# Strassen's seven products in place of eight, two blocks of 384 columns, in the second expert layer of a fused fp32 kernel

## The chip, the cores and the metric

The kernel runs on one core of a Trainium2 chip. The metric is the time of one execution on the device in microseconds (us). TensorE (PE in the rows, PEld for its weight loads) multiplies matrices into PSUM, which has eight banks here named bank_61 to bank_68; VectorE (DVE) and ScalarE (ACT) work element by element; GpSimd (POOL) does little here; SyncE (SP) issues all DMA transfers.

## The reference

Block-and-window attention over 2 x 768 tokens with 8 heads of 64 gives x of 1536 tokens by 512. Two dense layers follow, each with its own weights:

```python
def _moe_ref(x, w_in, w_out):            # w_in 512 x 2048, w_out 2048 x 512
    h = x @ w_in
    sp = np.where(h > 20.0, h, np.log1p(np.exp(np.minimum(h, 20.0))))
    return ((h * np.tanh(sp)) @ w_out).astype(np.float32)

def _moe2_ref(x, w_a, w_b, w_out):       # w_a, w_b 512 x 1536, w_out 1536 x 512
    a = x @ w_a
    b = x @ w_b
    return (a * b @ w_out).astype(np.float32)
```

All arithmetic is fp32. The weights arrive as 64-bit floats.

## The kernel before

Every fp32 product is made of three matmuls. Each operand is split into a rounded high part and a rest (`XH` and `XL` for x; high and low halves of a weight slot), and high x high, low x high and high x low are added up in PSUM. A split is always a ScalarE cast (the high part) and a VectorE subtraction (the rest).

The tokens stand in blocks 0 to 3 of 256, 256, 512 and 512 tokens; blocks 0 and 1 are mostly taken together, so a step handles 512 tokens. The layers' hidden columns are taken in chunks of 128: 16 for the first layer (`NC1`), 12 for the second (`NC2`). A visit is a token group with a range of chunks (`visits1`, `visits2`), and a step is one chunk of a visit. The stages run one after the other on TensorE: attention to about 84 us, mixed with the first visits; the first layer to about 335 us; then the second layer.

A step of the second layer (`step2`) computes a and b with 12 matmuls each: four pieces of the 512 input dimensions times three (line L811, in `x_product`). ScalarE copies a out of PSUM (L906), VectorE multiplies it with b, which it reads in PSUM (L907), ScalarE casts the product (L355, the line of the helper `copy`) and VectorE subtracts (L910). Two steps later 12 matmuls with w_out (L923) add the chunk to o, which stays in four PSUM banks for a whole visit and is copied or added at the visit's end (L944), and then stored. In the first layer L840 is the Mish activation, L843 its subtraction, and L858 the matmuls with w_out.

`load_w` fetches a weight tile of 128 x 512 (64-bit), and turns it into fp32 with integer instructions: ScalarE multiplies the high words by a power of two with Copy (L656), VectorE shifts the low words (L658), puts both together (L661) and puts in the sign (L664), and then the split follows (L355, L672). Each tile is converted once.

The order of all instructions is set before the program is built: `Plan.emit` takes the list of operations with their due times and estimated costs and puts out, engine by engine, the ready operation with the earliest key. On the chip each engine follows its own list, and semaphores hold it where data or a buffer isn't ready.

Of the kernel before, what the change touches and what calls it, by code (L numbers as in the profile page):

```python
# [232 lines left out]
def attention_mish_moe_bilinear_moe(  # L233
# [72 lines left out]
    RND = top[0]  # L306
    T_S = [take(512) for _ in range(NT)]
    T_L = [take(512) for _ in range(NT)]
    Y0, Y1 = take(KC * n_blk[0]), take(KC * n_blk[1])
    stage_o = [take(1024) for _ in range(NST)]  # L310
    SK = WIN + S + WIN
    kt_o = [take(SK) for _ in range(NP)]
    YP = [Y0, Y1, kt_o[0], None]
    assert kt_o[-1] + SK >= YP[2] + KC * n_blk[2]
    OP = [Y0, Y1, None, YP[2]]
# [15 lines left out]
    n_ext = max(top[0] - EXT, 1024 * N_EXT)  # L331
    assert EXT + n_ext <= TOT, EXT + n_ext
    ext_slots = [EXT + 1024 * i for i in range(n_ext // 1024)]
# [302 lines left out]
    free_slots = []  # L636
# [3 lines left out]
    def load_w(first, kind, c):  # L640
        free_slots.sort()
        t_free, o = free_slots.pop(0)
        w_at[kind, c] = o
        key = max(first - 9.0, t_free + 0.5)
        ext = [("ext",)] if o >= EXT else []
        _, so = nxt("stage", stage_o)
        kd = key - 4.0
        kd = w_dma.get((kind, c), kd)
        if BITS64:
            raw = ar(so, 512, 2)  # L650
            dma(kd, ar(so, 1024).bitcast(U32), w_dram[kind][c].bitcast(U32), w=[sb(so, 1024)],
                nbytes=P * 4096)
            f, hw = raw[:, :, 0], raw[:, :, 1]
# [4 lines left out]
            dve(key, 512, lambda env: nc.vector.tensor_scalar(  # L658
                out=f.bitcast(U32), in0=f.bitcast(U32), scalar1=29, scalar2=None,
                op0=ALU.logical_shift_right), fast=True, r=[sb(so, 1024)], w=[("f", so)])  # L660
            dve(key, 512, lambda env: nc.vector.scalar_tensor_tensor(  # L661
                out=f.bitcast(U32), in0=hw.bitcast(U32), scalar=3, in1=f.bitcast(U32),
                op0=ALU.logical_shift_left, op1=ALU.bitwise_or), r=[("hw", so), sb(so, 1024)], w=[("f", so)])
# [3 lines left out]
        else:  # L667
            f = ar(so, 512)
# [10 lines left out]
    def w_all(kind, c):  # L679
        o = w_at[kind, c]  # L680
        return lambda: (r32(ar(o + 512, 512)), r32(ar(o, 512)))

    def w_key(kind, c):
        return sb(w_at[kind, c], 1024)

# [323 lines left out]
```

## Time and profile before

| | |
|---|---|
| median of three runs | 630.74 us (630.29 to 633.08) |
| span of the profiled execution | 628.0 us; the page gives no other time for it |
| TensorE busy | 616.7 us, 98% |
| VectorE busy | 319.4 us, 51% |
| ScalarE busy | 263.1 us, 42% |
| second layer on TensorE | 335.41 to 623.74 us |

The span runs from the first to the last instruction of the profiled execution; a run's time is measured around the whole execution. A matmul's duration includes its way through the array, and matmuls overlap, so their pace is read from the starts. A row's duration of a VectorE or ScalarE instruction likewise overlaps a little with the next.

### The profile page before, as it was taken

To read this page: it belongs to the slowest core of one execution; us is meant where nothing else is said; L and a number is where in the kernel's file an instruction comes from. 1 tells how busy PE (TensorE), PEld (TensorE's weight loads), DVE (VectorE), ACT (ScalarE), POOL (GpSimd) and SP (SyncE) were. 2 spreads that over 40 slices of the span, in tenths; PEclk is the share of its full clock that TensorE was granted. 3 is DMA by queue.
4 is the path that set the end of the run, shared out by engine and by line. 5 is a ranking of instruction groups with operands and counts; after the bars stand their busy time and mean duration, and the time that the engine had idled before them with its cause. 6 is when DMAs were issued, how large, how long until landed. Compare 5 with 4: busy or idle time off the path is not lost.

```text
span 628.0 us, 9873 instructions
## 1 busy us (share of the span) xinstructions
PE 616.7 (98%) x3975; PEld 512.7 (82%) x3975; DVE 319.4 (51%) x741; ACT 263.1 (42%) x571; POOL 6.7 (1%) x34
## 2 busy tenths in 40 slices
PE   7899999999999999999999999999999999999997
PEld 4688988888888888888888888888888888888885
DVE  6989999998851311179898311115731111113112
ACT  5889989766632321256664112114521112111110
POOL 3000000000000000000000000000000000000000
PEclk8979999999999999999999999999999999999999
DMA  8997433445420000025542000002400001000101
GB/s 301 345 311 236 149 88 103 169 167 193 171 73 1 0 1 1 2 77 191 199 171 99 2 1 0 2 0 78 157 2 0 1 0 68 1 0 19 48 1 67
DMA packets 20633, 54.83 MB, mean 87 GB/s; under 512 B 1804, under 2 KB 4876, under 8 KB 20588
## 3 DMA queue, kind: packets, MB, share of 16 engines
q1 hardware_dynamic: 20588, 54.21, 25.2%
q8 instruction: 31, 0.51, 0.4%
q14 instruction: 14, 0.11, 0.1%
HBM read 50.07 MB, written 3.15 MB: 85 GB/s over the span
## 4 chain that ended last, share of the span: by engine, by line
PE 94%; ACT 4%; DMA 1%; issue 0%; DVE 0%; SPq 0%
PE bank L811 50%; PE bank L858 20%; PE bank L923 16%; PE bank L601 2%; PE bank L530 2%; PE bank L589 2%; ACT attn L557 2%; DMA attn<-in_qT_dram 1%; PE bank L534 1%; ACT rounded L355 0%; ACT arena L656 0%; ACT L840 0%; ACT L557 0%; PE bank L407 0%; PE bank L462 0%
## 5 line engine op out<-in xcount | busy, mean ns | idle before, releaser
L811 PE MATMUL bank<-rounded 128*128 128x512 f32 (+1 forms) x1068 | 239.1, 378 | 0.5 <-ACT arena L840 0.5
L811 PEld LDWEIGHTS bank<-rounded 128*128 128x128 f32 x1068 | 192.4, 188 | 38.1 <-ACT arena L840 0.7
L355 ACT CAST rounded<-arena 128x512 fp32r<-128x512 f32 (+1 forms) x131 | 81.1, 625 | 187.4 <-PE bank L923 125.9
L811 PE MATMUL bank<-rounded,wext 128*128 128x512 f32 x432 | 102.8, 389 | 0.0
L858 PE MATMUL bank<-rounded 128*128 128x512 f32 (+1 forms) x456 | 98.5, 364 | 0.0
L811 PEld LDWEIGHTS bank<-rounded,wext 128*128 128x128 f32 x432 | 81.1, 188 | 16.8
L907 DVE TENSOR_TENSOR arena<-arena,bank 128x512 f32<-128x512 f32 x36 | 24.7, 687 | 128.2 <-PE bank L811 128.1
L858 PEld LDWEIGHTS bank<-rounded 128*128 128x128 f32 x456 | 77.9, 189 | 13.7 <-issue 0.2
L843 DVE TENSOR_TENSOR rounded<-arena,rounded 128x512 fp32r<-128x512 f32 (+1 forms) x53 | 33.8, 637 | 72.6 <-ACT rounded L355 72.6
L923 PE MATMUL bank<-rounded 128*128 128x512 f32 x288 | 69.0, 389 | 0.0
L923 PEld LDWEIGHTS bank<-rounded 128*128 128x128 f32 x288 | 54.1, 188 | 11.2
L910 DVE TENSOR_TENSOR rounded<-arena,rounded 128x512 fp32r<-128x512 f32 x36 | 24.9, 692 | 66.3 <-ACT rounded L355 59.1
L656 ACT ACTIVATE arena<-arena 128x512 f32<-128x512 f32 x68 | 46.2, 684 | 16.2 <-DMA arena<-in_w_out_dram 7.6
L906 ACT COPY arena<-bank 128x512 f32<-128x512 f32 x36 | 21.2, 588 | 73.3 <-PE bank L811 73.3
L661 DVE SCALAR_TENSOR_TENSOR arena<-arena 128x512 uint32<-128x512 uint32 x68 | 47.0, 691 | 6.9 <-ACT arena L656 4.0
L840 ACT ACTIVATE arena<-bank 128x512 f32<-128x512 f32 (+1 forms) x53 | 29.4, 557 | 44.2 <-PE bank L811 44.0
L664 DVE SCALAR_TENSOR_TENSOR arena<-arena 128x512 uint32<-128x512 uint32 x68 | 46.9, 690 | 1.0
L858 PE MATMUL bank<-rounded,wext 128*128 128x512 f32 x180 | 43.2, 389 | 0.0
L557 ACT ACTIVATE attn<-attn 128x120 f32<-128x120 f32 x96 | 36.8, 385 | 8.7 <-DVE attn L551 8.6
L858 PEld LDWEIGHTS bank<-rounded,wext 128*128 128x128 f32 x180 | 33.8, 188 | 7.0
L672 DVE TENSOR_TENSOR rounded<-arena,rounded 128x512 fp32r<-128x512 f32 x47 | 32.2, 688 | 11.7 <-ACT rounded L355 11.4
L923 PE MATMUL bank<-wext,rounded 128*128 128x512 f32 x144 | 34.3, 389 | 0.0
(69 smaller groups left out, 385.7 us busy)
## 6 DMA issues: line engine op xcount, KB each, us to landing
arena<-in_w_out_dram SPq DMA_DIRECT2D x28, 512.0 KB, 3.4
arena<-in_w_in_dram SPq DMA_DIRECT2D x16, 512.0 KB, 3.7
arena<-in_w_a_dram SPq DMA_DIRECT2D x12, 512.0 KB, 3.2
arena<-in_w_b_dram SPq DMA_DIRECT2D x12, 512.0 KB, 3.3
arena<-in_kT_dram SPq DMA_DIRECT2D x8, 384.0 KB, 6.1
attn<-in_v_dram SPq DMA_DIRECT2D x4, 768.0 KB, 6.1
out_dram<-arena SPq DMA_DIRECT2D x12, 256.0 KB, 2.1
attn<-in_qT_dram SPq DMA_DIRECT2D x5, 512.0 KB, 6.1
```

The lines of the kernel that those rows point to most:

```text
L355: alts = [("ACT", act_us(n), lambda env: nc.scalar.copy(out=dst(env), in_=src(env))), ("DVE", dve2_us(n) if fast else dve_us(n), lambda en ...
L557: act(key, SW + 90, lambda env, x=x: nc.scalar.activation(out=s[:, x, :], in_=s[:, x, :], func=AF.Exp, scale=-1.0, bias=negm[:, x:x + 1], ...
L656: act(key, 512, lambda env: nc.scalar.activation(out=hw, in_=hw, func=AF.Copy, scale=2.0 ** -112), r=[sb(so, 1024)], w=[("hw", so)])
L661: dve(key, 512, lambda env: nc.vector.scalar_tensor_tensor(out=f.bitcast(U32), in0=hw.bitcast(U32), scalar=3, in1=f.bitcast(U32), op0=ALU. ...
L664: dve(key, 512, lambda env: nc.vector.scalar_tensor_tensor(out=f.bitcast(U32), in0=hw.bitcast(U32), scalar=0x80000000, in1=f.bitcast(U32), ...
L672: dve(key, 512, lambda env: nc.vector.tensor_sub(out=r32(ar(o, 512)), in0=f, in1=ar(o + 512, 512)), r=[sb(o + 512, 512), ("f", so), sb(so, ...
L811: nc.tensor.matmul(like(dst, b), lt, rt, start=(j == 0), stop=(j == 3 * KC - 1))
L840: act(ka, n, lambda env: nc.scalar.activation(out=g, in_=hp(env), func=AF.Mish), w=[hn, sb(lo, n)], free=[hn], table="mish")
L843: dve(ka, n, lambda env: nc.vector.tensor_sub(out=r32(gl), in0=g, in1=gh), r=[sb(lo, n), sb(ho, n)], w=[sb(go, n)])
L858: nc.tensor.matmul(yp, lt, r32(rt), start=(fst and j == 0), stop=(lst and j == 2))
L910: dve(ka, n, lambda env: nc.vector.tensor_sub(out=r32(gl), in0=pp, in1=gh), r=[sb(po, n), sb(ho, n)], w=[sb(ho + 512, n)])
L923: nc.tensor.matmul(bank[env[on]], lt, rt, start=(first and j == 0), stop=(last and j == 2))
```

## The change

The second layer no longer multiplies a and b apart. For one chunk, the 256 rows of (w_a, w_b) transposed times the 512 input dimensions form a 2 x 2 block matrix, and the x of 768 tokens (a block: A is tokens 0 to 767, B the rest) another one: two halves of the input dimensions by two sets of 384 tokens. The eight block products of an ordinary multiplication become seven (`SEQ`), each of two input pieces times three matmuls with 384 columns. For that, x is combined once for each block (`combine_x`), and the weights once for each chunk (`prep_w2`): sums and differences, each of which is split like the operands before. A group (`group`) is one chunk of one block: the seven products go into three PSUM banks X, Y and Z; between products ScalarE copies partial sums out of X and Z while later products are added to the same banks, and VectorE adds and multiplies in SBUF with the banks as one operand.

o is no longer kept in PSUM: `expand` multiplies one, two or three chunks with w_out, and each result is added into `X2` in SBUF (L1121) by VectorE, or copied there the first time. `plan2` is the written-out order of groups (B0 is chunk 0 of block B) and expansions (oB012). Weights go through three rotating buffers (`W2`, `O2`) and are prepared in time with their use. The first layer's last two visits are exchanged, so that block B is complete one visit earlier, and its results go to `X2`, not into `XH` and `XL`.

In the conversion of weights that are first used later than 20 us (of the planner's time) into the second layer, Prelu with alpha 2^32 takes the place of Copy, so that the high word carries the sign, and the or-step that puts in the sign (L697, L664 before) is left out. This holds for 27 of 68 tiles. With Prelu comes one more load of an activation table.

The diff, cut to its core:

```diff
+    X2 = [Y0 + KC * GT * i for i in range(6)]
+    TN = 384
+    tmp_o = [TMP + TN * i for i in range((T_L[-1] + 512 - TMP) // TN)]
...
+    W2 = [b0, e0, e0 + 3584]
+    O2 = [e0 + 7168 + 1024 * i for i in range(3)]
+    PH = [G_HL[0], G_HL[0] + 768] + [b0 + 3584 + 768 * i for i in range(3)] + [e0 + 10240]
...
+        if signed:
+            act(key, 512, lambda env: nc.scalar.activation(out=hw, in_=hw, func=AF.Prelu, scale=2.0 ** -112, alpha=2.0 ** 32),
+                r=[sb(so, 1024)], w=[("hw", so)], table="exp")
...
+    def prep_w2(c, key):
...
+        split(key + 0.2, fa, ra + ext, at(e + 512, 512), at(e, 512), 512)
+        split(key + 0.4, fb[:, 256:512], rb + ext, at(e + 1280, 256), at(e + 1024, 256), 256)
...
+        sm(key + 0.3, nc.vector.tensor_add, qa, fb[:, 0:256], fb[:, 256:512], rb + [sb(sa, 1024)], [("hw", sa)])
+        sm(key + 0.3, nc.vector.tensor_sub, qb, qa, fa[:, 0:256], ra, [("hw", sa)])
+        sm(key + 0.5, nc.vector.tensor_sub, ta, fa[:, 0:256], fb[:, 0:256], ra + rb, [("hw", sb_)])
+        sm(key + 0.5, nc.vector.tensor_sub, tb, fa[:, 256:512], qb, ra + [("hw", sa), sb(sb_, 1024)], [("hw", sb_)])
+        split(key + 0.4, ha, [("hw", sa), sb(sa, 1024)] + ext, at(e + 2048, 512), at(e + 1536, 512), 512)
+        split(key + 0.6, hb, [("hw", sb_), sb(sb_, 1024)] + ext, at(e + 3072, 512), at(e + 2560, 512), 512)
...
-    visits1 = [((0,), 0, NG1), ((1,), 0, NG1), ((2,), 0, NG1), ((3,), 0, NC1), ((0, 1), NG1, NC1), ((2,), NG1, NC1)]
-    visits2 = [((3,), 0, NG2), ((0, 1), 0, NG2), ((2,), 0, NC2), ((3,), NG2, NC2), ((0, 1), NG2, NC2)]
+    visits1 = [((0,), 0, NG1), ((1,), 0, NG1), ((2,), 0, NG1), ((3,), 0, NC1), ((2,), NG1, NC1), ((0, 1), NG1, NC1)]
...
+    plan2 = ["B0", "B1", "B2", "A0", "oB012", "A1", "A2", "A3", "oA012", "A4", "B3", "oA34", "B4", "B5", "oB34",
+             "B6", "A5", "oB56", "A6", "A7", "oA56", "A8", "B7", "oA78", "B8", "B9", "oB78", "Ba", "A9", "oB9a",
+             "Aa", "Ab", "oA9a", "Bb", "oAb", "oBb"]
...
+    def signed_w2(c):
+        return w_first[c] > t + 20.0
...
-    def step2(i, vi, b, c, ts, dt):
...
+    def combine_x(p_, key):
...
+        keep(key, "B11", b11)
+        keep(key + 0.1, "B21", b21)
+        minus(key + 0.2, b11, b12, b11)
+        keep(key + 0.4, "T1", b11)
+        minus(key + 0.6, b12, b22, b12)
+        keep(key + 0.6, "T3", b12)
+        keep(key + 0.7, "B22", b22)
+        minus(key + 0.3, b22, b22, b11)
+        keep(key + 0.3, "T2", b22)
+        minus(key + 0.8, b21, b21, b22)
+        keep(key + 0.8, "T4", b21)
...
+    SEQ = (("X", "A11", "B11", True), ("Y", "A12", "B21", True), ("X", "S2", "T2", False), ("Z", "S1", "T1", True),
+           ("X", "S3", "T3", False), ("Z", "S4", "B22", False), ("X", "A22", "T4", False))
...
+    def group(p_, c, ts):
...
+                for i in range(2):
+                    h, l = r32(ar(wh + i * P, P)), r32(ar(wl + i * P, P))
+                    xh, xl = r32(ar(hi[i], TN)), r32(ar(lo[i], TN))
+                    for j, (lt, rt) in enumerate(((h, xh), (l, xh), (h, xl))):
+                        nc.tensor.matmul(dst, lt, rt, start=(start and i == 0 and j == 0),
+                                         stop=(last and i == 1 and j == 2), skip_group_check=True)
...
+        product(0)
+        s1 = tmp()
+        out_of(ts + d, "X", s1)
+        product(1)
+        with_bank(ts + 2 * d, nc.vector.tensor_add, s1, "Y", True)
+        product(2)
+        s2 = tmp()
+        out_of(ts + 3 * d, "X", s2)
+        product(3)
+        s5 = tmp()
+        out_of(ts + 4 * d, "Z", s5)
+        product(4)
+        with_bank(ts + 5 * d, nc.vector.tensor_add, s5, "X")
+        product(5)
+        with_bank(ts + 6 * d, nc.vector.tensor_add, s2, "Z", True)
+        product(6)
+        with_bank(ts + 7 * d, nc.vector.tensor_mul, s1, "X", True)
+        dve(ts + 7 * d, TN, lambda env: nc.vector.tensor_mul(s2[0], s2[0], s5[0]), r=s5[1], w=s2[1])
...
+    def expand(p_, cs, ts):
...
+                if first:
+                    copy(kf, 512, lambda env, acc=acc: acc, lambda env, on=on: bank[env[on]], w=[on] + ak, free=[on])
                     continue
...
+                dve(kf, 512, lambda env, acc=acc, ot=ot, on=on: nc.vector.tensor_add(ot, bank[env[on]], acc),
+                    r=ak, w=[on] + ok, free=[on])
```

In the kernel after, line L1044 holds the matmuls of the groups, L1105 those of the expansions, L1052 ScalarE's copies out of X and Z (`out_of`), L1055 VectorE's instructions with a bank (`with_bank`), L1075 the product of the two halves, L705 every split's subtraction, L388 its cast, L736 the sums of weights, L1001 the differences of x, L690 and L693 the weights' conversion.

TensorE before, in the middle of the second layer: a step's two products into banks 64 and 66, then the matmuls of an earlier step with w_out into the four banks of o.

```order
L811 MATMUL bank3_64<-rounded_69 128x512 [waits Activation_49]
L811 MATMUL bank3_64<-rounded_69 128x512 x11
L811 MATMUL bank5_66<-rounded_69 128x512 [waits DVE_49]
L811 MATMUL bank5_66<-rounded_69 128x512 x11
L923 MATMUL bank0_61<-rounded_69 128x512 [waits Activation_49]
L923 MATMUL bank0_61<-rounded_69 128x512
L923 MATMUL bank0_61<-rounded_69 128x512 [waits DVE_49]
L923 MATMUL bank2_63<-rounded_69 128x512 x3
L923 MATMUL bank6_67<-rounded_69 128x512 x3
```

TensorE now, one group (chunk 7 of block A; X is bank 63, Y bank 67, Z bank 64): the fifth product is left out.

```order
L1044 MATMUL bank2_63<-rounded_69,wext_1756 128x384 x6
L1044 MATMUL bank6_67<-rounded_69,wext_1756 128x384 x6
L1044 MATMUL bank2_63<-rounded_69,wext_1756 128x384 [waits Activation_49]
L1044 MATMUL bank2_63<-rounded_69,wext_1756 128x384 x5
L1044 MATMUL bank3_64<-rounded_69,wext_1756 128x384 x6
...
L1044 MATMUL bank3_64<-rounded_69,wext_1756 128x384 [waits Activation_49]
L1044 MATMUL bank3_64<-rounded_69,wext_1756 128x384 x5
L1044 MATMUL bank2_63<-rounded_69,wext_1756 128x384 [waits DVE_49]
```

Before, the bank of a product was written again two steps later; now the third, fifth, sixth and seventh product each wait for an engine that reads the bank one product earlier.

VectorE in the same group, from the addition of Y (bank 67) to the addition of X (bank 63), for which the seventh product waits. The rows between are the preparation of later weights.

```order
L1055 TENSOR_TENSOR arena_70<-arena_70,bank6_67 128x384 [waits PE_49]
L736 TENSOR_TENSOR arena_70<-arena_70 128x256 [waits DVE_49]
L705 TENSOR_TENSOR wext_1756<-arena_70,wext_1756 128x512 [waits Activation_49]
L690 TENSOR_SCALAR arena_70<-arena_70 128x512 [waits DMAHW4_49]
L693 SCALAR_TENSOR_TENSOR arena_70<-arena_70 128x512 [waits DVE_49]
L1055 TENSOR_TENSOR arena_70<-arena_70,bank2_63 128x384 [waits PE_49,Activation_49]
```

In this place VectorE of the kernel before has only L907 and L910, one each for a step.

VectorE at the change from the first layer to the second: the last addition of the first layer's result (bank 68), the first addition of Y (bank 63, group B0), and the combination of block A's x, in front of the first addition from X (bank 61). Between the two pieces stand three more differences and three more subtractions.

```order
L970 TENSOR_TENSOR arena_70<-bank7_68,arena_70 128x2x256 [waits PE_49]
L1001 TENSOR_TENSOR arena_70<-arena_70 128x2x3x128 [waits DVE_49]
L1055 TENSOR_TENSOR arena_70<-arena_70,bank2_63 128x384 [waits PE_49,Activation_49]
...
L705 TENSOR_TENSOR rounded_69<-arena_70,rounded_69 128x768 [waits Activation_49]
L705 TENSOR_TENSOR rounded_69<-arena_70,rounded_69 128x768
L705 TENSOR_TENSOR rounded_69<-arena_70,rounded_69 128x2x384 [waits Activation_49]
L1055 TENSOR_TENSOR arena_70<-arena_70,bank0_61 128x384 [waits PE_49]
```

These subtractions are new at this place; before, the second layer's x was split piece by piece at the end of each visit. On TensorE twelve products of groups B0, B1 and B2 stand before the seventh product of B0.

## Rows read from the trace of the kernel before

**Rows 1.** The page's part 1: busy us, share, instructions of each engine.

```profile
PE 616.7 (98%) x3975; PEld 512.7 (82%) x3975; DVE 319.4 (51%) x741; ACT 263.1 (42%) x571; POOL 6.7 (1%) x34
```

**Rows 2.** Busy time by stretch: us; engines in the heading's order; PEclk, DMA share, GB/s.

```profile
core 0: us, PE busy (x) PEld busy (x) DVE busy (x) ACT busy (x) POOL busy (x), PEclk, DMA share, GB/s
335.41:623.74 288.33, 288.32 (x1273) 238.39 (x1271) 80.95 (x126) 63.55 (x106) 0.00 (x0) 1.00 0.07 25
623.74:628.00 4.26, 0.00 (x0) 0.00 (x0) 0.72 (x2) 0.00 (x0) 0.00 (x0) 0.82 0.56 207
```

**Rows 3.** The page's part 4: the chain that ended last, by engine.

```profile
PE 94%; ACT 4%; DMA 1%; issue 0%; DVE 0%; SPq 0%
```

**Rows 4.** Waits of TensorE's weight loads: us in total, times, longest.

```profile
PEld bank L811 <- ACT arena L840: 0.7, 1, 0.7
```

**Rows 5.** Groups by line and shape: busy us, mean ns | idle before.

```profile
L811 PE MATMUL bank<-rounded 128*128 128x512 f32 x948 | 223.3, 389 | 0.0
L811 PEld LDWEIGHTS bank<-rounded 128*128 128x128 f32 x1068 | 192.4, 188 | 38.1 <-ACT arena L840 0.7 <-DVE attn L551 0.4 <-ACT arena L656 0.2
...
L664 DVE SCALAR_TENSOR_TENSOR arena<-arena 128x512 uint32<-128x512 uint32 x68 | 46.9, 690 | 1.0
L656 ACT ACTIVATE arena<-arena 128x512 f32<-128x512 f32 x68 | 46.2, 684 | 16.2 <-DMA arena<-in_w_out_dram 7.6 <-DMA arena<-in_w_b_dram 4.3 <-DMA arena<-in_w_a_dram 3.3
...
L840 ACT ACTIVATE arena<-bank 128x512 f32<-128x512 f32 x43 | 25.6, 596 | 44.1 <-PE bank L811 44.0
...
L907 DVE TENSOR_TENSOR arena<-arena,bank 128x512 f32<-128x512 f32 x36 | 24.7, 687 | 128.2 <-PE bank L811 128.1
...
L906 ACT COPY arena<-bank 128x512 f32<-128x512 f32 x36 | 21.2, 588 | 73.3 <-PE bank L811 73.3
...
L811 PE MATMUL bank<-rounded 128*128 128x256 f32 x120 | 15.8, 287 | 0.5 <-ACT arena L840 0.5
...
L843 DVE TENSOR_TENSOR rounded<-arena,rounded 128x256 fp32r<-128x256 f32 x10 | 4.2, 418 | 0.0
L840 ACT ACTIVATE arena<-bank 128x256 f32<-128x256 f32 x10 | 3.8, 388 | 0.0
```

**Rows 6.** Timeline of TensorE: start us, us to the last end.

```profile
44.41 5.92 PE L811 MATMUL bank<-rounded 128*128 128x256 f32 x48
...
395.09 2.88 PE L923 MATMUL bank<-rounded 128*128 128x512 f32 x12
```

**Rows 7.** Timeline at three hand-overs: TensorE to ScalarE, to VectorE, ScalarE to TensorE.

```profile
391.24 1.29 PE L811 MATMUL bank<-rounded 128*128 128x512 f32 x5
...
392.57 0.59 ACT L906 COPY arena<-bank 128x512 f32<-128x512 f32 x1 [1.31 <-PE bank L811]
...
402.57 0.84 PE L811 MATMUL bank<-rounded,wext 128*128 128x512 f32 x3
...
403.52 0.69 DVE L907 TENSOR_TENSOR arena<-arena,bank 128x512 f32<-128x512 f32 x1 [4.39 <-PE bank L811]
...
59.66 0.38 ACT L840 ACTIVATE arena<-bank 128x256 f32<-128x256 f32 x1
...
60.09 1.49 PEld L811 LDWEIGHTS bank<-rounded 128*128 128x128 f32 x12 [0.67 <-ACT arena L840]
60.09 1.69 PE L811 MATMUL bank<-rounded 128*128 128x256 f32 x12 [0.47 <-ACT arena L840]
```

**Rows 8.** Timeline of VectorE, back to back.

```profile
317.74 0.69 DVE L672 TENSOR_TENSOR wext<-arena,wext 128x512 fp32r<-128x512 f32 x1
318.35 0.69 DVE L664 SCALAR_TENSOR_TENSOR arena<-arena 128x512 uint32<-128x512 uint32 x1
318.95 0.42 DVE L658 TENSOR_SCALAR arena<-arena 128x512 uint32<-128x512 uint32 x1
```

**Rows 9.** Busy time by stretch, as in rows 2.

```profile
20.00:40.00 20.00, 16.80 (x348) 14.28 (x344) 17.98 (x67) 16.82 (x53) 0.52 (x1) 0.83 0.99 336
...
280.00:340.00 60.00, 60.00 (x266) 49.68 (x265) 53.88 (x94) 37.45 (x62) 0.00 (x0) 1.00 0.48 167
```

More of the change, by code (lines that the diff above doesn't have):

```diff
@@ L306, in attention_mish_moe_bilinear_moe @@
     RND = top[0]
+    stage_o = [take(1024) for _ in range(NST)]
+    Y0, Y1 = take(KC * GT), take(KC * GT)
+    SK = WIN + S + WIN
+    kt_o = [take(SK) for _ in range(NP)]
     T_S = [take(512) for _ in range(NT)]
     T_L = [take(512) for _ in range(NT)]
[L309 to L315, printed above, removed]
+    X2 = [Y0 + KC * GT * i for i in range(6)]
+    assert Y1 == X2[1] and kt_o[0] == X2[2] and T_L[0] == T_S[0] + NT * 512
+    TMP = X2[5] + KC * GT
+    TN = 384
+    tmp_o = [TMP + TN * i for i in range((T_L[-1] + 512 - TMP) // TN)]
     EXT = -(-top[0] // CELL) * CELL
@@ L664, in load_w @@
+        if not signed:
             dve(key, 512, lambda env: nc.vector.scalar_tensor_tensor(
@@ L723, in attention_mish_moe_bilinear_moe @@
     first_use, last_use = {}, {}
-    for steps, kinds, late in ((steps1, ("in", "out"), "out"), (steps2, ("a", "b", "o2"), "o2")):
+    for steps, kinds, late in ((steps1, ("in", "out"), "out"),):
         for vi, b, c, ts, dt in steps:
@@ L777, in need @@
             load_w(first_use[kind, c], kind, c)
-    def release(steps, i, kinds):
-        c = steps[i][2]
-        if all(s[2] != c for s in steps[i + 1:]):
-            free_slots.extend((last_use[kind, c], w_at[kind, c]) for kind in kinds)
     def cut(offs, n, i=0):
@@ L847, in step1 @@
         ky = ts + 2.2 * dt
-        final = visits1[vi][2] == NC1
+        first_of = lambda b: min(v[1] for v in visits1 if set(v[0]) & set(b))
         for m in range(KC):
@@ L882, in step1 @@
-            act(kf, n, lambda env, m=m, src=src: nc.scalar.copy(out=r32(x_at(XH, b, m)), in_=src(env)),
-                r=sk, w=hk + bk)
-            dve(kf, n, lambda env, m=m, src=src: nc.vector.tensor_sub(
-                out=r32(x_at(XL, b, m)), in0=src(env), in1=x_at(XH, b, m)), r=hk + sk, w=lk + bk, free=done)
+                return like(bank[env[yn]][:, yo:yo + n], gran2[b])
+            part = len(gran2[b]) * GT == n and first_of(b) < visits1[vi][1]
+            xo = [X2[g] + m * GT for g in gran2[b]]
@@ new lines, in attention_mish_moe_bilinear_moe @@
+    combine_x(B_, vis_t[-2] + 2.0)
+    combine_x(A_, t - 2.0)
+    done_w, done_o = set(), set()
+    for o, p_, cs, ts in seq2:
+        if o:
+            for c in cs:
+                if c not in done_o:
+                    done_o.add(c)
+                    prep_o2(c, max(ts - 12.0, o_last[c - 3] + 0.5 if c >= 3 else 0.0))
+            expand(p_, cs, ts)
+            continue
+        for c in cs:
+            if c not in done_w:
+                done_w.add(c)
+                prep_w2(c, max(w_first[c] - 12.0, w_last[c - 3] + 0.5 if c >= 3 else w_first[c] - 40.0 + 8.0 * c))
+            group(p_, c, ts)
```

288 lines of the change are left out of this document (183 added, 105 removed).

## The prediction

> **What bounds the kernel now.** I read the page's share by engine first, then busy time by stage, then the chain of waits, and last single instructions. TensorE is busy 98% of the span [rows 1]. The stage that the change rewrites, the second expert layer, runs from 335.41 to 623.74 us; there the matmul row is busy for 288.32 of 288.33 us, while VectorE works 80.95 us and ScalarE 63.55 us [rows 2]. The chain that ended last is TensorE for 94% [rows 3], and over the whole kernel TensorE waited for a ScalarE result in front of line L811 only once, for 0.7 us [rows 4]. So this stage lasts as long as its matmuls: 24 of its 1296 (864 of L811, 432 of L923) stand before 335.41 us, and the other 1272 at 0.2267 us are 288.3 us. What the two other engines do is free until TensorE has to wait for it.
>
> **The matmuls.** The pace of a matmul is its start-to-start time. Twelve at 512 columns took 2.88 us from first start to last end, and one takes 0.389, so the pace is (2.88 - 0.389)/11 = 0.2265 us; 48 at 256 columns took 5.92 us, one takes 0.287, so it is (5.92 - 0.287)/47 = 0.120 us [rows 5, 6]. No row has 384 columns. Halfway between the two is 0.173 us. It cannot be quicker than the 0.120 of 256 columns; the slow bound is 0.188 us, what one weight load takes [rows 5], if loads could not run into each other. At 256 columns they do, as a pace of 0.120 with loads of 0.188 shows, so I take 0.173.
> Removed: 2 products x 12 chunks x 3 token groups x 12 matmuls = 864 at 0.2267 = 195.8 us. Added: 7 products x 6 matmuls x 12 chunks x 2 token blocks = 1008 at 0.1733 = 174.7 us. That is **-21.1 us** (-6.3 us at the slow bound). The 432 matmuls of the last product stay at 512 columns, and the first layer keeps its 1272.
> The rows fit columns/2.4 GHz plus 13 ns. The Trainium skill (TensorE: Matmul & The Clock Gate, Part 1, on 56 against 53.3 ns) has about 2.5 ns in place of the 13; by it the sum would be 864 x 215.8 - 1008 x 162.5 ns = 22.7 us saved. The trace does not agree, and 21.1 stands.
>
> **VectorE and ScalarE as a load.** Back to back, a 512-column VectorE instruction starts 0.61 us after the one before, though it lasts 0.69; the shift lasts 0.42, and with the same overlap of 0.08 its pace is about 0.34 [rows 8]. A column costs (687 - 418)/256 = 1.05 ns [rows 5], so 384 columns last 0.553 us at a pace of 0.475, 256 columns go at 0.34 and 768 at 0.88. In the stage after:
> 24 groups x 7 instructions x 0.475 = 80; 60 additions of o x 0.61 = 37; nine weight chunks prepared inside the stage (three shifts, three or-steps, four 512-column differences, five of 256 columns: 7.0 us) = 63; combining the x of block A (11 x 0.88 and four additions) = 12. Together 192 us; with 0.08 us more for each of the 378, as if each needed the one before it, 222. TensorE will need 288.3 - 21.1 = 267 us, so VectorE stands at 72 to 83%. In 280 to 340 us of this kernel it is busy 53.88 of 60 us and TensorE 60.00 [rows 9], so that load can be hidden; if it could not, the waits below are its price. ScalarE: 72 copies from PSUM (0.49 us by its two rows), 48 halves of the splits, 27 conversions (0.684), 52 casts, ten copies of o: about 120 us of 267.
> Prelu in place of Copy takes 27 of the 68 or-steps (0.690 us each) from VectorE. None lies on the path, so I cost it at nothing, as long as VectorE stays below TensorE. A Prelu has no row; Copy from SBUF has 0.684 and Mish from PSUM 0.596 [rows 5], and with either ScalarE is far from full.
>
> **The new waits.** This is where part of the gain goes. A group writes product 1 to bank X, product 2 to Y, then adds product 3 onto X, after ScalarE has copied X; products 5 and 6 wait for copies likewise, and product 7 for VectorE's addition from X. One product of six matmuls, 1.04 us, is all that lies between. A weight load is issued at the start of the matmul before its own, so the next product's is due 1.04 - 0.17 = 0.87 us after the writing product's turn ended. Against this: the last matmul's tail, (0.287 + 0.389)/2 - 0.173 = 0.165 us; then 0.04 us to ScalarE or 0.11 to VectorE; the copy 0.49 or the addition 0.55; and 0.05 back to TensorE [rows 5, 7]. ScalarE's way is 0.74 us, 0.13 to spare; VectorE's is 0.875, nothing to spare. So any other work in progress on these engines shows as a wait, plus about 0.1 us because the restarted load is no longer covered (twelve matmuls took 1.69 us after the wait where 11 x 0.120 + 0.287 = 1.61 [rows 7]).
> Bounds: nothing, if the engines are always free; and per group, with ScalarE busy 45% and VectorE 80% and half of a 0.69 us instruction left on average, 3 x 0.08 + 0.28 + 0.1 = 0.62 us, times 24 = 15 us. The order shown above says it is nearer the low end: between the addition of Y and that of X stand four others, 0.46 + 0.61 + 0.34 + 0.73 = 2.1 us, after 0.55 for the first, and products 3 to 5 give VectorE 3.12 us there; it is 0.4 us early (3.12 - 0.59 - 2.14). Behind a late X addition queue the additions of Z and the product of the halves, and after them the split that the last product reads, but that has at least one other group to spare. I take 0.25 us in the 18 groups that share VectorE with weight preparation and 0.05 in the last six: 5 us.
> At the change of stage, combining A's x (12 us, in the order above) stands in front of VectorE's first addition from X; twelve products (12.5 us) stand before the product that needs it. I add 1 us. **Waits: 6 us.** A wait of a quarter microsecond leaves TensorE about 98% busy; the granted clock was 0.83 where it was busy only 16.80 of 20 us [rows 9] and 1.00 all through this stage, so I charge nothing for the clock.
>
> **What costs nothing.** The order of the first layer is the same up to its last two visits, which swap. Preparing three chunks and block B's x then lies beside the last visit (11 steps of 24 matmuls, 60 us), where the kernel before converts 19 weight tiles with four VectorE instructions each, 76, against 18 for each of three chunks and 11 for x, 65. The same 36 weight tiles are loaded, by the same queue. The tail, 4.26 us from the last matmul to the end [rows 2], is again an addition and a store; VectorE's last six additions (0.61) keep up with TensorE's three matmuls each (0.68).
>
> **Sum.** The profiled execution has a span of 628.0 us and no other time; the runs shown have a median of 630.74, 2.7 more. 628.0 - 21.1 + 6 = 612.9 us of span, **615.6 us** as a run.
>
> **Rivals.**
> 1. Hardly any wait (under 3 us): 609.6 to 612.6. For it: the order leaves VectorE 0.4 us before the critical addition. Against it: no spare time in that addition's own round trip. 0.17.
> 2. The round trip decides. ScalarE and VectorE take their work in order, so a cast that waits for a late difference holds up the copy behind it, in every group. If each of the four waits finds a full 512-column instruction just begun, a group loses 3 x (0.69 - 0.13) + 0.69 + 0.4 = 2.8 us, 24 groups 67 us, and the run takes 677. It turns a gain into a loss from 21.1/24 = 0.88 us a group, a third of that; 10 to 18 us of waits (619.6 to 627.6) have 0.14, 18 to 24 us (no change) 0.04, more (slower, about 634 to 645) 0.05. For it: VectorE at 80%. Against it: the 90% above without a wait. The Trainium skill (Perfetto Trace Analysis, Optimizing Tensor Performance, Matmuls) wants independent groups to rotate through banks, so that reading one overlaps the next group, and larger matmuls; the change goes against both, and this rival is what that would do here.
> 3. The smaller product does not pay: weight loads set the pace at 0.188 us. Then 630.7 - 6.3 + 6 = 630.4, no change. For it: a load lasts longer than a 384-column matmul's pace. Against it: so it does at 256 columns. 0.05.
>
> **How the numbers follow.** The forecast (3 to 10 us of waits, 612.6 to 619.6) has 0.55. The range 610 to 625 takes in most of rival 1 and the nearer two thirds of rival 2's middle: about 0.8. Half a percent, 3.2 us, is about what a measurement here can tell from no change. Faster by more: 0.55 + 0.17 + 0.14 = 0.86; within it 0.04 + 0.05 = 0.09; slower 0.05.
>
> **What would show it.** Right: 1008 matmuls with a pace near 0.173 us; VectorE busy about 200 us in the stage; many short waits of L1044 for the copies of L1052 and the additions of L1055, 6 us in all, none in L1105. Wrong: a pace of 0.188; gaps of half a microsecond in every group; a clock below 1.00 in the stage; or a wait for weights, which would mean that preparing a chunk takes longer than the two groups it has.

## The result, and the profile after

The changed kernel takes 612.2 us (median of 4 runs, 611.44 to 612.6) against 631.91 us for the kernel before beside it: a ratio of 0.9686, interval 0.9657 to 0.9715. A second set gave 612.5 us and 0.9711 (0.9695 to 0.9727). It is 3% faster, within the range predicted, 3.4 us below the forecast; rival 1, hardly any wait, is the case that came, not the 3 to 10 us of waits that the forecast was made of.

The profiled execution has a span of 610.2 us, 17.8 less than before. First the page's part 1 of the changed kernel, which answers to [rows 1].

```profile
PE 597.1 (98%) x4119; PEld 525.4 (86%) x4119; DVE 411.2 (67%) x946; ACT 295.9 (48%) x648; POOL 6.8 (1%) x34
```

Next the busy time by stretch, as in [rows 2]. The first stretch is the whole second layer, from the first matmul of L1044 to the end of the last one of L1105; the second is the tail.

```profile
core 0: us, PE busy (x) PEld busy (x) DVE busy (x) ACT busy (x) POOL busy (x), PEclk, DMA share, GB/s
330.12:604.62 274.50, 274.49 (x1441) 256.04 (x1439) 194.95 (x368) 108.46 (x205) 0.00 (x0) 1.00 0.16 54
604.62:610.20 5.58, 0.00 (x0) 0.00 (x0) 0.78 (x2) 0.00 (x0) 0.00 (x0) 0.93 0.58 216
```

TensorE is still never idle in the layer by this view, at a granted clock of 1.00 (the 2.4 GHz level), while VectorE went from 80.95 to 194.95 us. The layer lasts 274.5 us; before it was 293.8 (1296 matmuls at 0.2267 us). That is 19.3 us less, and the tail gives 1.3 back (5.58 against 4.26 us). The chain that ended last, as in [rows 3]:

```profile
PE 90%; ACT 4%; DVE 2%; DMA 2%; issue 0%; SPq 0%; DVEq 0%; ACTq 0%
```

The waits of TensorE's weight loads in the layer, as in [rows 4] (total us, times, longest). This one line is all that the view has there.

```profile
PEld bank L1044 <- ACT arena L1052: 0.5, 3, 0.2
```

The groups of the new work by line and shape, as in [rows 5].

```profile
L1044 PE MATMUL bank<-rounded,wext 128*128 128x384 f32 x672 | 120.4, 335 | 0.0
L1044 PEld LDWEIGHTS bank<-rounded,wext 128*128 128x128 f32 x672 | 117.1, 188 | 1.3 <-ACT arena L1052 0.5
L1105 PE MATMUL bank<-wext,rounded 128*128 128x512 f32 x360 | 87.4, 390 | 0.0
L1055 DVE TENSOR_TENSOR arena<-arena,bank 128x384 f32<-128x384 f32 x96 | 52.6, 551 | 39.5 <-PE bank L1044 30.4 <-ACT arena L685 4.0 <-ACT wext L388 2.2
L1052 ACT COPY arena<-bank 128x384 f32<-128x384 f32 x72 | 34.3, 481 | 53.9 <-PE bank L1044 51.7 <-DVE rounded L705 2.0
L688 ACT ACTIVATE arena<-arena 128x512 f32<-128x512 f32 x41 | 27.9, 686 | 6.2 <-DMA arena<-in_w_out_dram 2.4 <-DMA arena<-in_w_b_dram 1.6 <-DMA arena<-in_w_a_dram 1.5
L685 ACT ACTIVATE arena<-arena 128x512 f32<-128x512 f32 x27 | 18.3, 681 | 18.7 <-DMA arena<-in_w_a_dram 8.9 <-DMA arena<-in_w_out_dram 5.9 <-DMA arena<-in_w_b_dram 3.8
```

The releasers to look at are those of L1055 and L1052: both engines wait for TensorE (30.4 and 51.7 us), not it for them. The pace is in the chain, told in order of time (start us, us, what).

```profile
330.26 28.16 PE bank L1044 x162
358.43 12.28 PE bank L1105 x54
370.71 21.89 PE bank L1044 x126
```

28.16/162 and 21.89/126 are both 0.174 us; the commonest distance between two starts at 384 columns is 0.173.

Where the prediction's 6 us of waits should have stood, the timeline of the changed kernel shows this (start us, us, and in brackets the idle time before and what ended it).

```profile
438.68 3.80 PE L1044 MATMUL bank<-rounded,wext 128*128 128x384 f32 x20
438.96 2.04 PEld L1044 LDWEIGHTS bank<-rounded,wext 128*128 128x128 f32 x12
...
439.38 0.47 ACT L1052 COPY arena<-bank 128x384 f32<-128x384 f32 x1
...
440.61 0.48 ACT L1052 COPY arena<-bank 128x384 f32<-128x384 f32 x1
...
441.15 1.01 PEld L1044 LDWEIGHTS bank<-rounded,wext 128*128 128x128 f32 x6 [0.15 <-ACT arena L1052]
```

This is one of the three waits: a copy held up by a cast, and a load that the view has idle for 0.15 us. The row of 20 matmuls shows no break, but by its starts the matmul behind the waiting one comes 0.10 us late. Only four matmul starts in the layer are more than 0.03 us late, 0.35 us in all. The tail has two rows, of VectorE and of SP's queue.

```profile
598.29 7.87 SPq L375 DMA_DIRECT2D out_dram<-arena  x12
...
605.11 0.69 DVE L1121 TENSOR_TENSOR arena<-bank,arena 128x512 f32<-128x512 f32 x1 [0.40 <-DMA out_dram<-arena]
```

All twelve stores leave in the last 12 us (before, four in the last 6), and the last addition waits 0.40 us for a staging buffer that a store still reads.

### The profile page after: what moved, and what is told of

Same layout as the page of the kernel before. It is cut to its first block, busy times and chain, and to the rows that moved or that the text cites. A ratio compares the mean times of both kernels' runs of the same rounds, so it can differ in the third digit from the quotient of the medians.

```text
span 610.2 us, 10411 instructions
## 1 busy us (share of the span) xinstructions
PE 597.1 (98%) x4119; PEld 525.4 (86%) x4119; DVE 411.2 (67%) x946; ACT 295.9 (48%) x648; POOL 6.8 (1%) x34
## 4 chain that ended last, share of the span: by engine, by line
PE 90%; ACT 4%; DVE 2%; DMA 2%; issue 0%; SPq 0%; DVEq 0%; ACTq 0%
PE bank L1044 29%; PE bank L950 21%; PE bank L903 20%; PE bank L1105 16%; PE bank L634 2%; ACT attn L590 2%; PE bank L563 1%; PE bank L622 1%; DMA attn<-in_qT_dram 1%; ACT arena L688 1%; PE bank L567 1%; DMA out_dram<-arena 1%; ACT rounded L388 1%; DVE attn L584 0%; ACT L932 0%
## 5 line engine op out<-in xcount | busy, mean ns | idle before, releaser
L388 ACT CAST rounded<-arena 128x512 fp32r<-128x512 f32 (+3 forms) x139 | 82.4, 606 | 93.0 <-PE bank L950 40.3
L1044 PE MATMUL bank<-rounded,wext 128*128 128x384 f32 x672 | 120.4, 335 | 0.0
L1044 PEld LDWEIGHTS bank<-rounded,wext 128*128 128x128 f32 x672 | 117.1, 188 | 1.3 <-ACT arena L1052 0.5
L950 PE MATMUL bank<-rounded 128*128 128x512 f32 (+1 forms) x456 | 98.0, 364 | 0.0
L903 PE MATMUL bank<-rounded 128*128 128x512 f32 (+1 forms) x456 | 96.0, 363 | 0.5 <-ACT arena L932 0.5
L903 PEld LDWEIGHTS bank<-rounded 128*128 128x128 f32 x456 | 77.6, 189 | 14.4 <-ACT arena L932 0.7
L950 PEld LDWEIGHTS bank<-rounded 128*128 128x128 f32 x456 | 77.9, 189 | 13.7 <-issue 0.2
L1105 PE MATMUL bank<-wext,rounded 128*128 128x512 f32 x360 | 87.4, 390 | 0.0
L1055 DVE TENSOR_TENSOR arena<-arena,bank 128x384 f32<-128x384 f32 x96 | 52.6, 551 | 39.5 <-PE bank L1044 30.4
L1105 PEld LDWEIGHTS bank<-wext,rounded 128*128 128x128 f32 x360 | 67.4, 188 | 13.4
L705 DVE TENSOR_TENSOR rounded<-arena,rounded 128x512 fp32r<-128x512 f32 (+3 forms) x92 | 59.4, 658 | 5.7 <-ACT rounded L388 4.0
L1044 PE MATMUL bank<-rounded 128*128 128x384 f32 x336 | 61.1, 335 | 0.0
L1052 ACT COPY arena<-bank 128x384 f32<-128x384 f32 x72 | 34.3, 481 | 53.9 <-PE bank L1044 51.7
L1044 PEld LDWEIGHTS bank<-rounded 128*128 128x128 f32 x336 | 58.7, 188 | 0.6
L388 ACT CAST wext<-arena 128x512 fp32r<-128x512 f32 (+2 forms) x62 | 37.7, 615 | 43.3 <-DVE arena L1075 11.0
L693 DVE SCALAR_TENSOR_TENSOR arena<-arena 128x512 uint32<-128x512 uint32 x68 | 47.0, 691 | 6.6 <-ACT arena L688 2.2
L1121 DVE TENSOR_TENSOR arena<-bank,arena 128x512 f32<-128x512 f32 x60 | 40.4, 687 | 14.1 <-PE bank L1105 13.5
L903 PE MATMUL bank<-rounded,wext 128*128 128x512 f32 x180 | 43.2, 389 | 0.0
L950 PE MATMUL bank<-rounded,wext 128*128 128x512 f32 x180 | 43.2, 389 | 0.0
L705 DVE TENSOR_TENSOR wext<-arena,wext 128x512 fp32r<-128x512 f32 (+2 forms) x62 | 38.7, 634 | 5.1 <-PE bank L950 2.5
```

What stands on the lines that cost most here:

```text
L388: alts = [("ACT", act_us(n), lambda env: nc.scalar.copy(out=dst(env), in_=src(env))), ("DVE", dve2_us(n) if fast else dve_us(n), lambda en ...
L693: dve(key, 512, lambda env: nc.vector.scalar_tensor_tensor(out=f.bitcast(U32), in0=hw.bitcast(U32), scalar=3, in1=f.bitcast(U32), op0=ALU. ...
L705: dve(key, n, lambda env: nc.vector.tensor_sub(out=r32(lo[0]()), in0=src, in1=hi[0]()), r=rd + hi[1], w=lo[1])
L903: nc.tensor.matmul(like(dst, b), lt, rt, start=(j == 0), stop=(j == 3 * KC - 1))
L950: nc.tensor.matmul(yp, lt, r32(rt), start=(fst and j == 0), stop=(lst and j == 2))
L1044: nc.tensor.matmul(dst, lt, rt, start=(start and i == 0 and j == 0), stop=(last and i == 1 and j == 2), skip_group_check=True)
```

## The experiments

Theory A is that the whole gain is matmul time, because the new round trips from bank to bank stay hidden; against it stand several rivals, told run by run. All spans stand against 610.2 us.

**Eight plain products instead of seven.** Same 384 columns, same output.

```diff
-    SEQ = (("X", "A11", "B11", True), ("Y", "A12", "B21", True), ("X", "S2", "T2", False), ("Z", "S1", "T1", True),
-           ("X", "S3", "T3", False), ("Z", "S4", "B22", False), ("X", "A22", "T4", False))
+    SEQ = (("X", "A11", "B11", True), ("X", "A12", "B21", False), ("Y", "A11", "B12", True), ("Y", "A12", "B22", False),
+           ("Z", "A21", "B11", True), ("Z", "A22", "B21", False), ("V", "A21", "B12", True), ("V", "A22", "B22", False))
```

> The seven products of a group become the eight plain block products at the same 384 columns (same output): no sums of weights, no combinations of x, and no bank that is written again after a read. Theory A (the gain is the eighth product left out, and nothing else in the seven-product form costs time): 24 x 6 x 0.1735 = 25.0 us more matmul time, less the 0.5 us of waits, so 636 to 637.5 us, slower than the kernel before by some 4 us (1152 x 0.1735 - 864 x 0.2267 = 4.0). Rival B (the sums, combinations and read-backs of the seven-product form cost TensorE several us): at most 633 us.

635.52 us, 1.0073 of the kernel before (1.0049 to 1.0097), span 633.5: half a microsecond below theory A's range and 2.5 us above the most that rival B gave. Busy time of the second layer in this kernel:

```profile
330.00:628.50 298.50, 298.50 (x1586) 280.89 (x1584) 135.98 (x238) 86.66 (x161) 0.00 (x0) 1.00 0.14 50
```

The layer is 24.0 us longer than with seven products. The eighth product alone is 25.0, so everything that the seven-product form costs TensorE (sums, combinations, read-backs, 59 us more of VectorE) is 1.0 us. Theory A holds but for that microsecond. The run also shows the two halves of the change: cutting 512 columns to 384 costs 4.7 us (298.5 against 293.8), leaving out every eighth product wins 24.0.

**No Prelu.**

```diff
     def signed_w2(c):
-        return w_first[c] > t + 20.0
+        return False
```

> One part undone: no Prelu, so all 36 second-layer weight conversions take four VectorE steps instead of 9 with four and 27 with three. VectorE gets 27 x 0.61 = 16.5 us more in the second layer (195.6 us busy there now, of 274). Theory A (the time comes from TensorE's matmuls alone, and VectorE's round trips stay hidden because the order puts them first): 611 to 614 us, span within 1.5 us of 610.2. Rival B (VectorE's relief was needed): more waits of L1044, at least 3 us more, 615 us or above.

613.29 us, 0.9719 (0.9697 to 0.9742), span 610.3. The layer took 275.5 us, 1.0 more, with four waits (1.9 us of weight loads) instead of three (0.5). VectorE was busy 208.68 us there. In time it is not to be told from the changed kernel: theory A. The microsecond is the difference of two traces.

**The swap of visits alone, in the kernel before.**

```diff
-    visits1 = [((0,), 0, NG1), ((1,), 0, NG1), ((2,), 0, NG1), ((3,), 0, NC1), ((0, 1), NG1, NC1), ((2,), NG1, NC1)]
+    visits1 = [((0,), 0, NG1), ((1,), 0, NG1), ((2,), 0, NG1), ((3,), 0, NC1), ((2,), NG1, NC1), ((0, 1), NG1, NC1)]
```

> The kernel before with only the last two visits of the first layer swapped. Theory A: the same time as the kernel before, within 0.3%, 630 to 634 us. Rival C (part of the gain comes from the first layer's new order): 2 us or more faster.

630.57 us, 1.0001 (0.9985 to 1.0018): nothing, as theory A says.

**The critical addition twice.** In this run, the next two and the load unknown to the order, the engines' order is that of the changed kernel but for the repeated instructions.

```diff
+            twice = z == "X" and not free
...
+                if twice:
+                    op(out=r32(ar(EX, TN)), in0=dst[0], in1=bank[env[nm[z]]][:, 0:TN])
                 op(out=dst[0], in0=dst[0], in1=bank[env[nm[z]]][:, 0:TN])
```

> Same order of every engine as the changed kernel; only VectorE does each group's addition from bank X (between products 5 and 7) twice, the first time into a scratch. So VectorE's way from bank to bank gets 0.475 us longer in 24 places. In the trace of the changed kernel 16 of the 24 have one product between and the next load 0.053 us behind the addition, nothing to spare. Theory A (the round trip just fits, place by place): 16 x (0.475 to 0.575) = 7.6 to 9.2 us more, 620 to 621.5 us, waits of L1044 for L1055 half a microsecond each. Rival B (VectorE, 71% busy in the second layer, has time to spare, so an extra 11.4 us is hidden): 612 to 613.5 us. Rival D (a late addition carries on to what is queued behind it): 627 us or more.

621.52 us, 0.9865 (0.9846 to 0.9884), span 619.1: 8.9 more. The waits of weight loads:

```profile
PEld bank L1045 <- DVE arena L1061: 9.9, 18, 0.8
PEld bank L1045 <- ACT arena L1053: 1.5, 4, 0.6
```

Theory A met, rivals B and D out: VectorE was idle for 80 us of the changed kernel's layer, and its idle time still did not hide 11 us of extra work in these places: the layer got 9.6 us longer.

**The same with 16 columns**, to see how much such a way may grow.

```diff
-                    op(out=r32(ar(EX, TN)), in0=dst[0], in1=bank[env[nm[z]]][:, 0:TN])
+                    op(out=r32(ar(EX, 16)), in0=dst[0][:, 0:16], in1=bank[env[nm[z]]][:, 0:16])
```

> Same order of every engine as the changed kernel; in front of each group's addition from bank X VectorE adds 16 of its columns into a scratch, so that its way from bank to bank gets some 0.10 to 0.20 us longer (a VectorE instruction of 512 columns goes at a pace of 0.61 and one of 256 at 0.34, so 16 columns at about 0.09; behind the doubled addition the second one started 0.11 later than its pace). Theory G (a load may be late by its lead of 0.17 us before its matmul is): the matmuls lose at most 0.1 us in each of 16 groups, stage at most 1.5 us longer than 274.5, 612 to 614 us. Theory H (the prediction's: nothing to spare on VectorE's way, and a wait costs 0.1 us more for the restart): 16 x (0.20 to 0.30) = 3.2 to 4.8 us more, 615 to 617.5 us.

614.34 us, 0.9735 (0.9708 to 0.9762), span 612.6; the layer took 277.2 us, 2.7 more: between the two theories. The timeline shows the short addition, the real one behind it and the load that waits for it, and the view of waits what loads waited.

```profile
481.35 0.17 DVE L1060 TENSOR_TENSOR rounded<-arena,bank 128x16 fp32r<-128x16 f32 x1 [1.70 <-ACT rounded L388]
481.56 0.55 DVE L1061 TENSOR_TENSOR arena<-arena,bank 128x384 f32<-128x384 f32 x1
...
482.16 1.00 PEld L1045 LDWEIGHTS bank<-rounded 128*128 128x128 f32 x6 [0.19 <-DVE arena L1061]
```

```profile
PEld bank L1045 <- DVE arena L1061: 3.3, 16, 0.3
```

The addition starts 0.21 us later. In almost all of these places the start times of the matmuls show two late ones: the first by 0.04 us, the next by 0.107 more. 16 x 0.15 = 2.4 us is most of the 2.7; the rest is one copy that came 0.4 us later than in the changed kernel. Theory G forgot that the following matmul is held up too, theory H that a load runs ahead of its matmul.

The starts of loads and matmuls at 384 columns show why, and all these traces fit one rule. A load on time starts together with the matmul before its own, 0.171 us ahead of its own. Behind a late load the next one starts 0.108 us later, and the matmul of that next one 0.171 us after it. So from a late load to the start of the second matmul it takes 0.279 us, where from a load on time it takes two paces, 0.346. That leaves about 0.06 us free, and lateness beyond it is lost: up to 0.17 us by the second matmul alone, above that by both. How late the load starts, and what the two matmuls lose together:

| load late, us | lost, us | where |
|---|---|---|
| 0.06 | 0.005 | doubled copies (next run) |
| 0.10 | 0.03 | changed kernel, at 356 us |
| 0.165 | 0.10 | changed kernel, the wait at 441 us |
| 0.21 | 0.15 | 16 columns |
| 0.30 | 0.24 | doubled copies |
| 0.59 | 0.53 | doubled additions |

In the doubled addition the second one starts 0.59 later (484.46 and 485.05 us in one group); 14 of the places lose 0.53 us each.

**Each copy out of a bank twice.**

```diff
+                for o in (r32(ar(EX, TN)), dst[0]):
-            nc.scalar.copy(out=dst[0], in_=bank[env[nm[z]]][:, 0:TN])
+                    nc.scalar.copy(out=o, in_=bank[env[nm[z]]][:, 0:TN])
```

> Same order of every engine as the changed kernel; only ScalarE does each of the 72 copies out of a bank twice, the first time into a scratch, 0.40 us more each. In the trace of the changed kernel 58 have one product between, and most leave 0.19 us from the copy's end to the next load, of which the hand-over takes 0.05: 0.14 us to spare. Theory A: 58 x (0.26 to 0.36) = 15 to 21 us more, 627 to 633 us. Rival B (ScalarE, 40% busy, hides it): 612 to 613.5 us. Rival D (a late copy makes VectorE's additions late too, which have no spare time): 635 us or more.

622.27 us, 0.9882 (0.9865 to 0.9898), span 620.3: 10.1 more, 9.3 of them in the layer, where theory A had 15 to 21.

```profile
PEld bank L1045 <- ACT arena L1055: 11.2, 38, 0.6
```

Again the engine's idle time does not hide it (ScalarE is busy 39% of the changed kernel's layer), so rival B is out, and rival D too. Theory A's size was off for two reasons. The second copy starts 0.375 us later, so with 0.14 to spare its load should be 0.24 late, and with 0.06 free that costs 0.18, not 0.26 or more: six places show this. In most others the first copy itself starts 0.055 us later behind the last matmul than in the changed kernel, which these rows do not explain; the load is 0.30 late there, and 0.24 us are lost. And only 38 of the 58 places wait: in 16, the load six matmuls before was late, that gave the copy time, and its own load is only 0.05 to 0.06 us late and costs next to nothing.

**More work on VectorE, unknown to the order, and known to it.** `times` is 2 in the preparation of w_a, w_b and w_out2; the last pair of lines of the diff is in the second kernel alone.

```diff
         def fn(env):
+            for _ in range(times):
                 nc.vector.tensor_sub(out=r32(lo[0]()), in0=src, in1=hi[0]())
...
-        dve(key, n, fn, r=rd + hi[1], w=lo[1])
+        dve(key, n * times, fn, r=rd + hi[1], w=lo[1])
```

> Same order of every engine as the changed kernel, but each difference of the second layer's weight preparation (60 instructions) is done twice by VectorE, at times of which the order knows nothing: 12 x (4 x 0.61 + 0.34) = 33 us more, VectorE 229 of 274 us, 83%. Theory A (the waits are absent because of where the additions stand in the order, not because VectorE has time to spare): in 6 to 12 of the groups a doubled difference now stands in front of an addition with nothing to spare, 0.6 us each, 4 to 8 us more, 616 to 620 us. Rival B (spare time alone): 612 to 613.5 us.

> The same 33 us of extra differences as in the run with the load that the order did not know of, but the order is made with their true cost. Theory A: the additions are placed ahead again, 612 to 614 us, at least 2 us below the other. Rival B (spare time alone): no difference between the two. Rival E (83% is too much however it is placed): both 616 us or more.

626.77 us (0.9953, 0.9935 to 0.997; span 624.6, with another 2.5 us of waits at the end of the first layer) and 618.57 us (0.9819, 0.9802 to 0.9836; span 616.8). Both are above what theory A gave. The waits of weight loads in the layer, first with the load unknown to the order:

```profile
PEld bank L1049 <- ACT arena L1057: 7.6, 12, 1.7
PEld bank L1049 <- DVE arena L1060: 5.2, 5, 2.1
```

and with the load known to it:

```profile
PEld bank L1049 <- ACT arena L1057: 4.4, 8, 0.9
PEld bank L1049 <- DVE arena L1060: 1.4, 3, 0.6
```

The order is worth 8.2 us (6.5 in the layer, the rest mostly at the end of the first one), so rival B falls; but knowing the load does not hide it, so theory A fell in its strong form and rival E is nearer. The waits are now mostly ScalarE's copies, though no work was added to ScalarE. The timeline of the kernel whose order knows the load shows how:

```profile
463.96 0.70 ACT L685 ACTIVATE arena<-arena 128x512 f32<-128x512 f32 x1 [2.08 <-DMA arena<-in_w_a_dram]
...
464.89 0.52 ACT L388 CAST wext<-arena 128x384 fp32r<-128x384 f32 x1 [0.23 <-DVE arena L1080]
...
465.50 0.69 ACT L685 ACTIVATE arena<-arena 128x512 f32<-128x512 f32 x1
...
466.10 0.50 ACT L388 CAST rounded<-arena 128x384 fp32r<-128x384 f32 x1
...
466.50 0.46 ACT L1057 COPY arena<-bank 128x384 f32<-128x384 f32 x1
...
467.01 0.64 PEld L1049 LDWEIGHTS bank<-rounded,wext 128*128 128x128 f32 x4 [0.73 <-ACT arena L1057]
```

ScalarE waited 2.08 us for a transfer and 0.23 for VectorE, then had two conversions and a cast to do before the copy that TensorE needed. That is rival 2's mechanism in kind: ScalarE works in order, and the copy stands behind other work, here conversions that a transfer made late.

**Reads of a bank first.** The kernel whose order knows the load, with the keys of its copies and additions 20 us earlier.

```diff
-            act(k, TN, lambda env: nc.scalar.copy(out=dst[0], in_=bank[env[nm[z]]][:, 0:TN]), w=[nm[z]] + dst[1])
+            act(k - 20.0, TN, lambda env: nc.scalar.copy(out=dst[0], in_=bank[env[nm[z]]][:, 0:TN]), w=[nm[z]] + dst[1])
...
-            dve(k, TN, lambda env: op(out=dst[0], in0=dst[0], in1=bank[env[nm[z]]][:, 0:TN]),
+            dve(k - 20.0, TN, lambda env: op(out=dst[0], in0=dst[0], in1=bank[env[nm[z]]][:, 0:TN]),
```

> The kernel with 33 us of extra differences whose order knows their cost (6.6 us more span than the changed kernel, 10 waits of L1049 for copies and additions), but the copies and additions that read a bank get a key 20 us earlier, so that in the order they go ahead of weight preparation whenever they are ready. Theory F (its waits come from preparation placed ahead of the reads): waits below 2 us, 613 to 615 us. Rival E (the order had placed them well; at 83% VectorE and ScalarE run behind the times that the order assumed, and what is in progress cannot be put aside): less than 2 us gained, 616.5 to 618.5 us.

616.8 us, 0.9777 (0.9759 to 0.9796), span 615.7: 1.1 less than without, inside rival E's range. 4.9 us of weight loads waited instead of 5.8, far above theory F's 2. But the keys changed more than was meant: they also drew groups of the second layer in between the last steps of the first (its first matmul starts at 312.3 us, without them at 332.2), so TensorE's order is another one, and the run does not show what earlier reads alone would do. By the two traces nothing was gained at all: of the 1.1 us, 0.8 lie within the first 62 us, before anything that the keys touch, and 0.3 in the tail; the matmuls in between take 549.3 us in both.

**Another end, alone and with the earlier keys**, with the changed kernel run again beside them.

```diff
-        for h in range(2):
-            for g in range(3):
+        hg = [(h, g, 0, 512) for h in ((1, 0) if final else (0, 1)) for g in range(3)]
...
+                if final and p_ == A_ and SPREAD:
+                    ko = ts - GD + 0.5 + 1.5 * i if i < 4 else ts + (i - 4) * OD / 6
...
-                if final:
-                    oo = nxt("ost", O_ST)[1]
-                    ot, ok = ar(oo, 512), [sb(oo, 512)]
```

> The changed kernel once more, as the measure for the three kernels beside it: 0.9686 of the kernel before, 610 to 612.5 us.

> The changed kernel with another end: the last additions of o stay in place and are stored from there (no staging buffer to wait for), four of block A's last six expansions are spread between the last group's products, block B's half that is ready first is expanded first, and the last expansion is cut into two of 256 columns. In the trace of the changed kernel the tail behind the last matmul is 5.59 us against 4.26 before [rows 2]: the last addition starts 0.46 us late for a staging buffer, and the last store takes 2.9 us instead of 2.1 behind the others. Theory A (those two are the tail's excess): 1.0 to 1.8 us less, a tail near 4 us. Rival (the end of the program sets the tail, not the stores): within 0.4 us of the changed kernel.

> The changed kernel with the new end and with the earlier keys for the reads of a bank: a trial of a better version. Theory A (in the changed kernel hardly any wait is left that a key could remove): the same as the kernel with the new end alone, within 1 us. Theory F: up to 1 us faster than that one.

612.5, 612.09 and 613.86 us; 0.9711 (0.9695 to 0.9727), 0.9717 (0.9696 to 0.9737) and 0.9734 (0.9717 to 0.9751); spans 610.4, 609.5 and 612.1. The tail of the kernel with the new end alone:

```profile
604.46:609.50 5.04, 0.04 (x1) 0.00 (x0) 1.10 (x3) 0.00 (x0) 0.00 (x0) 0.86 0.65 233
```

0.56 us shorter than in the rerun (5.60) and about half of the least that theory A had: no addition waits for a buffer now, but the two half stores at the end take 0.41 and 0.43 us to issue, one behind the other. The kernels above that kept the old end, but whose last addition happened to find its buffer free, have a tail of 4.7 to 5.1 us as well, so the new end is worth that wait and no more. By the runs it is no change. The earlier keys made it no better: weight loads waited 0.9 us in the layer (here too groups moved in between the first layer's steps), and at 60 us into the span its matmuls stood 1.1 us behind those of the new end alone. No version beats the changed kernel by more than these runs can tell.

## Why the prediction was right, and what was off

**The matmuls** came as predicted: 1008 at 0.1733 us and 432 at 0.2267 are 272.6 us, and the layer lasted 274.5. The weight-load bound of 0.188 (rival 3) did not come, though loads of 188 ns stand in every row. The Trainium skill (TensorE: Matmul & The Clock Gate, Part 1) gives, as an estimate with its 2.5 ns, 162.5 ns for 384 columns; the trace has 173 and does not agree. That the gain is the missing product, and not the swap or Prelu, is shown by three runs.

**The load** was right as well: 194.95 us of VectorE against 192 to 222, with hardly a loss of its own; ScalarE's 108 are a tenth below the 120. **Prelu at nothing**: right (681 ns, against 686 for Copy, and one microsecond in the layer between two traces).

**The waits** were the mis-sized term: 6 us taken, 1.9 measured (274.5 less 272.6), of which the view of waits has 0.5. The forecast itself, 3 to 10 us of waits, did not come; the time lies in the range because the range took in rival 1, which had 0.17. Of the signs of being right, "many short waits, 6 us in all" failed. The rest of the 1.9 is not waiting that any view names: some 110 of the layer's matmul starts come 5 to 30 ns late, together 1.0 us; the kernel before has none such, the eight-product kernel some too.

The step that failed is "any other work in progress on these engines shows as a wait", taken at 0.25 us in each of 18 groups. There hardly was any work in progress: in the trace 45 of 58 copies start 0.04 us and 15 of 16 additions 0.11 us after the last matmul, that is at once. The pair of runs with extra load shows that the order decides this: unknown to the order, the same load cost 8.2 us more. "VectorE's is 0.875, nothing to spare" was nearly right: in the changed kernel the load in 15 of 16 such places starts 0.053 us after the addition, so it does wait for it, and only some 0.06 us more would be free (about 0.20 on ScalarE's way). "Plus about 0.1 us" for the restart was wrong: a late load costs its lateness less 0.06, not more. The extra microsecond for the change of stage was not there either; the three waits stand at 441, 461 and 507 us.

**The tail** was taken as unchanged and cost 1.3 us more. In kernels with the same end whose last addition found its staging buffer free it cost 0.5 to 0.8 (tails of 4.7 to 5.1 us), so the wait for that buffer is about half of the 1.3. What the rest comes from, with twelve stores leaving together instead of four, no run took apart. **From span to run** the prediction added 2.7 us; every kernel run here took 1.7 us longer than its span, the kernel with swapped visits too (628.9 and 627.2), so a microsecond of the 2.7 was the spread of the runs before.

By steps, the span: 329.97 + 278.6 + 4.26 = 612.8 forecast (612.9 in the prediction, by rounding), 330.12 + 274.50 + 5.58 = 610.2 found. So part of the nearness is luck: 4.1 us too much for waits and 1.0 from span to run, 1.3 too little for the tail.

**Rival 2** did not happen, but its mechanism is real. With VectorE's share of the layer at 71% the loads waited 0.5 us, at 76% (no Prelu, 208.68 us) 1.9, at 79% (221.0 us, with an order made for it) 5.8, and at 78% with an order not made for it 12.8. Each of these kernels but the last has an order of its own, so the share alone is not shown to be the cause. The advice of the Trainium skill (Perfetto Trace Analysis, Optimizing Tensor Performance, Matmuls) to rotate independent groups through banks is what the eight-product run does inside a group, with no bank written again after a read: it saved 1.0 us of the 25 it cost.

## What to carry to other kernels

When TensorE is the bound, count its matmuls at the pace of their shape first; work moved to idle engines is free as long as no matmul waits for a particular instruction. For such a wait compare the way from bank to bank with the work in between plus the little that a late weight load may cost nothing (0.06 us here), and see from the order whether the reader is free at that moment: the engine's busy share says little about one place (at 78 and 79% the loads of two kernels waited 12.8 and 5.8 us). Lengthen a suspected way by a known small amount in a run of its own; that measures the spare time, which rows of single instructions did not give.

## Not expected of the hardware

A load may be late by about 0.06 us, although it starts 0.171 us ahead of its matmul: behind a late load the next starts 0.108 us later, though a load lasts 0.188, and it is this next load's matmul that loses first. An addition of 16 columns lasts 0.17 us and holds the next up by 0.21, so short instructions on such a way are not cheap. The two reads of a doubled pair start 0.59 us apart on VectorE and 0.375 on ScalarE. Why single matmuls start 5 to 30 ns late stays open.
